# A layer norm, linear attention and gated MLP on one core: the first stage with column halves, another order of loads, and four h chunks begun on two token tiles

## The chip, the core and the metric

The kernel runs on one core of a Trainium2 chip. The metric is the device time of one execution in microseconds. Seven runs of the kernel before gave a median of 143.49 us, from 143.22 to 143.72.

## The reference

x has 2048 tokens of 448 features, all in bfloat16. The function normalises each token and sends the result through two branches. Branch A is linear attention with 16 heads of 28 features. Branch B is an MLP with 1792 hidden features and a squared ReLU. The output is x plus A times the SiLU of B.

```python
def _layernorm(x, axis=-1, eps=1e-5):
    m = jnp.mean(x, axis=axis, keepdims=True)
    v = jnp.var(x, axis=axis, keepdims=True)
    return (x - m) / jnp.sqrt(v + eps)
...
    qkv = (xn @ wqkv).reshape(B, S, 3, H, Dh)      # H = 16, Dh = 28
    phi = lambda t: jnp.where(t > 0, t + 1, jnp.exp(t)) + 1e-6
    pq, pk = phi(q), phi(k)
    kv = jnp.einsum("bhsd,bhse->bhde", pk, v)
    z = jnp.einsum("bhsd->bhd", pk)
    num = jnp.einsum("bhqd,bhde->bhqe", pq, kv)
    den = jnp.einsum("bhqd,bhd->bhq", pq, z)[..., None] + 1e-6
    s = (num / den).reshape(B, S, D) @ wo
...
    h = xn @ w1 + b1
    h = jnp.where(h > 0, h, 0) ** 2
    g = silu(h @ w2 + b2)
    return x + s * g
```

## The kernel before

**Tiles.** The 2048 tokens are 16 tiles of 128, in four groups of 512. The 448 features lie in four chunks of 128, 128, 128 and 64. Matmuls contract over features, so the normalised x (`xn`, tokens on partitions) is turned into `xT` (features on partitions). The last 64 features stand twice, on partitions 0 to 63 and 64 to 127, so that the half-height step of one product can run on either half of TensorE beside a step of another product. For this, `xn` has 512 columns: a copy, the twin (`ln_twin`, L477), puts columns 384 to 447 again into 448 to 511.

**Products of the first stage.** K is a product for one token tile (`kk`, matmuls at L597): 128 tokens by 512 of the columns of wqkv, from the k columns and the last of q. Q is one chunk of 128 q columns by a group of 512 tokens (`qq`, L628). H is one of 14 chunks of 128 hidden features by a group of 512 tokens (`hh`, L640). Each collects in one PSUM bank of 512 float32 columns, of which there are eight. K and Q go through phi: an Exp on ScalarE (L575) and two VectorE operations (L578, L585). H goes through ReLU with bias on ScalarE (L649) and a square on VectorE or ScalarE (L657, L658). `pe_four` runs four products in pairs of half-height matmuls, one of the pair on partitions 0 to 63 and the other on 64 to 127. Seven such half-height steps make one product, since the four chunks hold seven halves.

**Order of the work.** The program lists operations with what they read and write. `schedule` places them in planned time, and `emit` writes out one instruction stream for each engine, with semaphore waits for the true dependences and for reuse of PSUM banks. TensorE and SP keep the order of the program. ScalarE, VectorE and POOL take what can start soonest; among those near in start, the one with the smallest `late` goes first. `late` is the latest planned start, less `lead` for a DMA, or `prio` where it is set by hand. At run time each engine executes its stream strictly in order, so an instruction that waits holds all that stand behind it.

**The head.** Group 0 has its own code. `load_x(0, 1, "act")` issues the first x tile on ScalarE's queue, `load_x(1, 2)` the second on SP, and `load_x(2, 4, "act")` tiles 2 and 3 on ScalarE's queue. The weights for K (`load_k`: one main part for the first three chunks, two small rests for the fourth chunk and its copy) go on SP behind tile 1, then w1 columns 0 to 511 (`w1a`), x tiles 4 to 7, `w1b`, wq, `w1c`. The bias b1 is loaded as 14 rows of 128 on ScalarE's queue, and the activation table is loaded there after the DMA issues. Each tile then passes statistics (L444), aggregate (L447), Ln and Exp on ScalarE (L455, L459), which make the reciprocal deviation `rstd`, and the norm (L466). Priorities give VectorE the order in `order` (L996).

TensorE first runs ten matmuls of 512 columns on a zeroed tile `junk` (`warm`). `pe_transpose` turns a whole tile with five transposes and one copy out of PSUM, by ScalarE for tiles 0 and 2 and by VectorE for 1 and 3. `pe_two` gives the full-height steps of K0 and K1, then the transposes of tiles 2 and 3, then the two half-height rests of K0 and K1. b1 is turned after that, and `quads` starts with H0 H1 H2 H3:

```python
        streams = (
            ("H0 H1 H2 H3 K2 H4 K3 H6", "H5 Q0 Q1 H7 H8 H9 Q2 H11 H10 K0' H12 H13"),
```

K0' is the K product of tile 4, the first of the next group. Tiles 4 to 15 are turned by transposing DMAs on SP (`dma_transpose`, L505), and x of tiles 8 to 11 is loaded between those of tiles 5 and 6.

**Behind the first stage** come the last H products, the sums over tokens, the folds of the small matrices, and the second products with w2 and the attention output, group by group (L905, L971); the change edits none of it.

Of the kernel before, what the change touches and what calls it, by code (L numbers as in the profile page):

```python
# [9 lines left out]
P = 128  # L10
# [7 lines left out]
RATE = 262e3  # L18
LEAD = 8.0
# [13 lines left out]
class Op:  # L33
    def __init__(self, eng, emit, reads, writes, dur, alts, nbytes):
        self.eng, self.emit, self.dur, self.alts, self.nbytes = eng, emit, dur, alts, nbytes
        self.reads, self.writes = list(reads), list(writes)
        self.raw, self.deps, self.succ = set(), set(), []
        self.start = self.end = None
        self.seq = None
        self.late = 1e9  # L40
        self.lead = LEAD
        self.prio = None
        self.sync = set()
# [10 lines left out]
class Program:  # L54
# [3 lines left out]
    ENGINES = ("pe", "act", "dve", "pool", "sp")  # L58
# [27 lines left out]
    def schedule(self):  # L86
# [25 lines left out]
        free["pool"] = free["dve"] = 0.8  # L112
# [7 lines left out]
        def ready(op):  # L120
            r = 0.0
            for d in op.deps:
                if d.end is None:
                    return None
                r = max(r, d.end + (0.0 if d.eng == op.eng == "pe" and d not in op.sync else LAT))
            return r
# [14 lines left out]
        while n:  # L141
# [69 lines left out]
            if op.nbytes:  # L211
                free[e] = st + op.dur
                s2 = max(dma_free, st + 1.9)
                dma_free = s2 + op.nbytes / RATE
                op.end = dma_free + 0.7
            else:
                op.end = st + du
                free[e] = op.end
# [62 lines left out]
def bass_recurrent_scan__linear_attn_block__dense_activation_squared_relu__prompt_kernel(  # L281
    nc, A_x, A_wqkv, A_wo, B_x, B_w1, B_b1, B_w2, B_b2, out
):
    with ExitStack() as es:
# [5 lines left out]
        junk = sb("junk", [P, 512], bf)  # L290
# [14 lines left out]
        b1r = sb("b1r", [NF, P], bf)  # L305
# [33 lines left out]
        def pool(fn, writes, reads=(), dur=0.3):  # L339
            add("pool", fn, reads, writes, dur)  # L340
# [4 lines left out]
        add("dve", lambda e, _: e.memset(junk[:, :], 0.0), [], ["junk"], 0.2).prio = -1000  # L345
# [29 lines left out]
        pool(lambda e, _: e.memset(zmask[:, :, :], 1.0), ["zmask"])  # L375
# [22 lines left out]
        def load_k(eng, w, src, name, lo, hi, eng2=None):  # L398

            n = (hi - lo) * 2  # L400
            dma(
                eng, w[:, 0:3, lo:hi], src[0:384, lo:hi].rearrange("(c p) j -> p c j", p=P), [(name, 0)], 384 * n
            )
            for i in (0, 1):
                dma(eng2 or eng, w[64 * i : 64 * i + 64, 3, lo:hi], src[384:448, lo:hi], [(name, 1 + i)], 64 * n)

# [13 lines left out]
        load_x(0, 1, "act")  # L420
        load_x(1, 2)
        load_k("sp", w_qkv, A_wqkv, "wk", 384, 2 * D)
        load_x(2, 4, "act")
        dma("act", b1r[:, :], B_b1.rearrange("(f p) -> f p", p=P), ["b1r"], F * 2).prio = -103
# [5 lines left out]
        add("act", lambda e, _: e.preload_act_table_set("natural_log_exp_and_others"), [], ["actw"], 1.3).prio = -101  # L430

# [10 lines left out]
        def ln_stats(si, prio=(None, None)):  # L442
            add(
                "dve", lambda e, _: e.bn_stats(st6[:, si, :], x_tok[:, si, :]), [("x", si)], [("st", si)], 0.553  # L444
            ).prio = prio[0]
            add(
                "dve", lambda e, _: e.bn_aggr(mv[:, si, :], st6[:, si, :]), [("st", si)], [("mv", si)], 0.16  # L447
            ).prio = prio[1]

        def ln_rstd(lo, hi):  # L450
            c = slice(lo, hi)
            ts = range(lo, hi)
            add(
                "act",
                lambda e, _: e.activation(out=vep[:, c], in_=mv[:, c, 1], func=AF.Ln, bias=eps5[:, 0:1]),  # L455
                [("mv", i) for i in ts] + ["eps5", "actw"], [("vep", i) for i in ts], 0.2,
            )
            add(
                "act", lambda e, _: e.activation(out=rstd[:, c], in_=vep[:, c], func=AF.Exp, scale=-0.5),  # L459
                [("vep", i) for i in ts], [("rstd", i) for i in ts], 0.2,  # L460
            )

        def ln_norm(si, prio=None):
            add(
                "dve",
                lambda e, _: e.tensor_scalar(  # L466
                    out=xn[:, si, 0:D], in0=x_tok[:, si, :], scalar1=mv[:, si, 0:1],
                    scalar2=rstd[:, si : si + 1], op0=ALU.subtract, op1=ALU.mult,
                ),
                [("x", si), ("mv", si), ("rstd", si)], [("xn", si)], 0.43,  # L470
            ).prio = prio

        def ln_twin(lo, hi):

            ts = range(lo, hi)
            add(
                "dve", lambda e, _: e.tensor_copy(xn[:, lo:hi, 448:512], xn[:, lo:hi, 384:448]), [("xn", i) for i in ts],  # L477
                [("xd", i) for i in ts], 0.1 + 0.03 * (hi - lo),
            )

        def pe_transpose(si, eng, prio):
            b = Buf("T")

            def f(e, _):
                v = ps(b)[:, :].bitcast(bf)
                for c in range(3):
                    e.transpose(v[:, c * P : (c + 1) * P], xn[:, si, c * P : (c + 1) * P], ident[:, :])  # L487
                e.transpose(v[0:64, 3 * P : 4 * P], xn[:, si, 384:448], ident[:, :])  # L488
                return e.transpose(v[64:P, 3 * P : 4 * P], xn[:, si, 384:448], ident[:, :])

            add("pe", f, [("xn", si), "ident"], [b], 0.35)

            def ev(e, _):
                src = ps(b)[:, 0:256].bitcast(bf).rearrange("p (c k) -> p c k", c=4)
                dst = xT[:, :, si * P : (si + 1) * P]
# [4 lines left out]
            add(eng, ev, [b], [("xT", si)], 0.42 if eng == "dve" else 0.6).prio = prio  # L500

        def dma_transpose(si):
# [5 lines left out]
            op.lead = LEAD + STAGGER * (3 - si % 4)  # L508
# [43 lines left out]
        def pe_two(a, b, between):  # L552

            for u in (a, b):

                def f(e, _, u=u):
                    for k in range(3):
                        last = u.mm(e, 2, k, k == 0, False)
                    return last

                add("pe", f, u.reads, [u.bank], 3 * MM(u.n))
            between()

            def rest(e, _):
                a.mm(e, 0, 3, False, True)
                return b.mm(e, 1, 3, False, True)

            add("pe", rest, [r for u in (a, b) for r in [*u.reads, u.bank]], [a.bank, b.bank], MM(a.n) + 0.1)
            a.out()
            b.out()  # L570
# [20 lines left out]
        def kk(si):  # L591
# [10 lines left out]
            return Acc(b, [("xT", si)] + wnames("wk"), mm, lambda: phi(b, qk_of(si), ("pk", si), blocks), 512)  # L602
# [21 lines left out]
        def qq(g, m):  # L624
# [8 lines left out]
            reads = [("xT", 4 * g + i) for i in range(4)] + wnames("wq")  # L633
            return Acc(b, reads, mm, lambda: phi(b, pqT[:, m, g * 512 : (g + 1) * 512], ("pq", g, m), lambda a: a), 512)

        def hh(g, fi):
            b = Buf("H")

            def mm(e, h, c, start, stop):
                return e.matmul(  # L640
                    ps(b)[:, 0:512], w_1[half[h], c, fi * P : (fi + 1) * P], xT[half[h], c, g * 512 : (g + 1) * 512],
# [3 lines left out]
            def out():  # L645
# [9 lines left out]
                def sq(e, eng):  # L655
                    if eng == "dve":
# [5 lines left out]
            return Acc(b, [("xT", 4 * g + i) for i in range(4)] + wnames(w1_of(fi)), mm, out, 512)  # L662
# [333 lines left out]
        order = ["st0", "mv0", "st1", "mv1", "xn0", "st2", "xn1", "mv2", "st3", "mv3", "xT1", "xn2", "xn3", "xT2", "xT3"]  # L996
        at_head = {n: -100 + i for i, n in enumerate(order)}
        for si in range(4):
            ln_stats(si, (at_head[f"st{si}"], at_head[f"mv{si}"]))
            ln_rstd(si, si + 1)  # L1000
            ln_norm(si, at_head[f"xn{si}"])

        def warm(n, after=(), wide=False):
            b = Buf("W")

            def f(e, _):
                last = None
                for _i in range(n):
                    w = 512 if wide else P
# [3 lines left out]
            add("pe", f, ["junk", *after], [b], n * (0.426 if wide else 0.107))  # L1013
            return b

        warm(10, wide=True)
        pe_transpose(0, "act", -100)
        warm(2)
        pe_transpose(1, "dve", at_head["xT1"])

        def third_and_fourth():
            pe_transpose(2, "act", -100)
            pe_transpose(3, "dve", at_head["xT3"])

        pe_two(kk(0), kk(1), third_and_fourth)
        bb = Buf("B1")
        add(
            "pe", lambda e, _: e.transpose(ps(bb)[:, 0 : NF // 2].bitcast(bf), b1r[:, :], ident[0:NF, 0:NF]),
            ["b1r", "ident"], [bb], 0.1,
        )  # L1030
        add(
            "act", lambda e, _: e.activation(out=b1f[:, :], in_=ps(bb)[:, 0 : NF // 2].bitcast(bf), func=AF.Copy), [bb],
            ["b1f"], 0.25,
        )

        def quads(g, what):
# [11 lines left out]
            ("H0 H1 H2 H3 K2 H4 K3 H6", "H5 Q0 Q1 H7 H8 H9 Q2 H11 H10 K0' H12 H13"),  # L1048
# [4 lines left out]
        for g, (first, second) in enumerate(streams):  # L1053
            if g + 1 < NG:
                ln(4 * g + 4, 4 * g + 8)
            quads(g, first)
# [91 lines left out]
```

## Time and profile before

| | |
|---|---|
| median of seven runs | 143.49 us |
| the profiled execution, whole time | 143.22 us |
| the profiled execution, span | 142.0 us |
| TensorE busy | 137.8 us, 97% of the span |
| VectorE busy | 91.3 us, 64% |
| ScalarE busy | 78.7 us, 55% |
| x tile of 112 KB, ScalarE's queue and SP's, issue to landing | 2.7 and 2.6 us |
| x tiles 2 and 3, 224 KB, issue to landing | 3.8 us |
| K weights, main part of 384 KB; rests of 64 KB | 4.2 us; 4.1 us |
| w1a, main part of 384 KB | 4.1 us |
| first statistics start | 3.57 us |
| first transposes of tiles 0, 1, 2, 3 start | 5.49, 6.32, 8.10, 8.54 us |
| first matmul of K0 | 6.77 us |
| first matmul of H0 | 9.59 us |
| first matmul of K2 | 12.62 us |

Times inside the execution count from the start of the span. The whole time is longer than the span by what lies around the program's instructions. Busy time is the sum over an engine's instructions; a busy engine may still be off the path that sets the end. The granted clock of TensorE was full in all 40 slices of the span.

### The profile page before, as it was taken

To read this page: it belongs to the slowest core of one execution; us is meant where nothing else is said; L and a number is where in the kernel's file an instruction comes from. 1 tells how busy PE (TensorE), PEld (TensorE's weight loads), DVE (VectorE), ACT (ScalarE), POOL (GpSimd) and SP (SyncE) were. 2 spreads that over 40 slices of the span, in tenths; PEclk is the share of its full clock that TensorE was granted. 3 is DMA by queue.
4 is the path that set the end of the run, shared out by engine and by line. 5 is a ranking of instruction groups with operands and counts; after the bars stand their busy time and mean duration, and the time that the engine had idled before them with its cause. 6 is when DMAs were issued, how large, how long until landed. Compare 5 with 4: busy or idle time off the path is not lost.

```text
span 142.0 us, 3024 instructions
## 1 busy us (share of the span) xinstructions
PE 137.8 (97%) x1215; PEld 67.3 (47%) x1215; DVE 91.3 (64%) x218; ACT 78.7 (55%) x151; POOL 23.4 (17%) x37
## 2 busy tenths in 40 slices
PE   6999999999999999999999999999999999999992
PEld 2344444444444444444445455654555555555482
DVE  0979698698897999678959900149852436052743
ACT  3667979889878898879799572143030211030220
POOL 6000000000000000000790000000050507350670
PEclk9999999999999999999999999999999999999999
DMA  4998958999251300000000025990001110201022
GB/s 108 323 329 241 96 157 279 342 242 132 55 42 37 74 18 5 0 9 14 0 0 0 0 78 143 191 174 12 5 7 58 37 32 32 97 28 41 32 97 67
DMA packets 19809, 12.90 MB, mean 91 GB/s; under 512 B 9364, under 2 KB 19412, under 8 KB 19796
## 3 DMA queue, kind: packets, MB, share of 16 engines
q1 hardware_dynamic: 17644, 11.22, 33.2%
q10 hardware_dynamic: 2152, 1.50, 4.5%
q8 instruction: 9, 0.15, 0.4%
q14 instruction: 4, 0.03, 0.1%
HBM read 8.78 MB, written 2.10 MB: 77 GB/s over the span
## 4 chain that ended last, share of the span: by engine, by line
PE 93%; DVE 3%; DMA 2%; issue 0%; DVEq 0%
PE pb L905 30%; PE pb L640 30%; PE pb L597 8%; PE pb L971 8%; PE pb L672 6%; PE pb L628 6%; DMA x_tok<-in_A_x_dram 2%; DVE st L444 1%; PE pb L678 1%; PE pb L765 1%; PE pb L726 1%; PE pb L487 1%; PE pb L803 0%; DVE xn L466 0%; PE pb L488 0%; DVE xT L497 0%
## 5 line engine op out<-in xcount | busy, mean ns | idle before, releaser
L640 PE MATMUL pb<-xT,w 64*128 64x512 bf16 x392 | 50.8, 376 | 0.1
L905 PE MATMUL pb<-w,r 64*128 64x448 bf16 (+3 forms) x378 | 45.1, 343 | 0.0
L649 ACT ACTIVATE r<-pb,b1f 128x512 bf16<-128x512 f32 x56 | 34.9, 689 | 4.1 <-PE pb L640 4.1
L640 PEld LDWEIGHTS pb<-xT,w 64*128 64x128 bf16 x392 | 21.4, 94 | 23.3 <-ACT r L649 0.6
L905 PEld LDWEIGHTS pb<-w,r 64*128 64x128 bf16 (+1 forms) x378 | 22.7, 95 | 20.0 <-issue 1.2
L916 DVE TENSOR_TENSOR gbuf<-pb,b2b 128x448 bf16<-128x448 f32 (+1 forms) x16 | 9.3, 609 | 33.2 <-PE pb L905 33.2
L881 ACT ACTIVATE gbuf<-gbuf 128x448 bf16<-128x448 bf16 (+1 forms) x16 | 8.6, 564 | 37.1 <-DVE gbuf L916 34.4
L950 POOL TENSOR_TENSOR xn<-xn,x_tok 128x448 bf16<-128x448 bf16 x15 | 15.1, 1030 | 48.7 <-DVE xn L941 48.7
L597 PE MATMUL pb<-w_qkv,xT 64*128 64x512 bf16 (+1 forms) x106 | 17.6, 377 | 0.0
L628 PE MATMUL pb<-xT,w_qkv 64*128 64x512 bf16 x84 | 15.5, 376 | 0.0
L657 DVE TENSOR_TENSOR r<-r 128x512 bf16<-128x512 bf16 x38 | 13.2, 418 | 0.0
L382 POOL MEMSET kvm<- 128x2048 bf16 x1 | 1.8, 1804 | 64.9 <-DVE zb L622 64.9
L971 PE MATMUL pb<-msb,pqT 64*128 64x448 bf16 (+3 forms) x93 | 11.2, 343 | 0.0
L444 DVE BATCH_NORM_STATS2 st<-x_tok 128x6 f32<-128x448 bf16 x16 | 9.4, 612 | 2.4 <-DMA x_tok<-in_A_x_dram 2.4
L575 ACT ACTIVATE qk<-pb 128x512 bf16<-128x512 f32 x16 | 9.0, 594 | 3.3 <-PE pb L597 2.7
L585 DVE SCALAR_TENSOR_TENSOR qk<-pb,qk 128x512 bf16<-128x512 f32 x16 | 10.7, 687 | 0.2
L941 DVE TENSOR_TENSOR xn<-pb,gbuf 128x448 bf16<-128x448 f32 (+2 forms) x17 | 9.3, 590 | 1.9 <-ACT gbuf L881 1.5
L658 ACT ACTIVATE r<-r 128x512 bf16<-128x512 bf16 x18 | 10.4, 651 | 0.0
L597 PEld LDWEIGHTS pb<-w_qkv,xT 64*128 64x128 bf16 (+1 forms) x106 | 6.6, 94 | 6.5 <-DVE xT L497 0.3
L672 PE MATMUL pb<-qk,xn 128*128 128x448 bf16 x48 | 9.4, 352 | 0.0
L628 PEld LDWEIGHTS pb<-xT,w_qkv 64*128 64x128 bf16 x84 | 6.0, 94 | 5.0
L616 DVE TENSOR_TENSOR zacc<-zacc,qk 128x448 f32<-128x448 f32 x13 | 8.1, 622 | 0.3
(81 smaller groups left out, 98.6 us busy)
## 6 DMA issues: line engine op xcount, KB each, us to landing
out_dram<-xn SPq DMA_DIRECT2D x15, 112.0 KB, 1.7
w<-in_B_w_dram SPq DMA_DIRECT2D x1, 1568.0 KB, 9.6
x_tok<-in_A_x_dram SPq DMA_DIRECT2D x3, 448.0 KB, 4.2
w<-in_B_w_dram SPq DMA_DIRECT2D x2, 384.0 KB, 4.6
xT<-rows ACTq DMA_DIRECT2D x6, 112.0 KB
w<-in_B_w_dram SPq DMA_DIRECT2D x1, 576.0 KB, 5.5
xT<-rows SPq DMA_DIRECT2D x5, 112.0 KB
w_o<-in_A_wo_dram SPq DMA_DIRECT2D x1, 392.0 KB, 10.7
```

What stands on the lines that cost most here:

```text
L444: "dve", lambda e, _: e.bn_stats(st6[:, si, :], x_tok[:, si, :]), [("x", si)], [("st", si)], 0.553
L585: lambda e, _: e.scalar_tensor_tensor(out=slot, in0=src(), scalar=1.0 + 1e-6, in1=slot, op0=ALU.add, op1=ALU.max),
L597: return e.matmul(ps(b)[:, 0:512], xT[half[h], c, si * P : (si + 1) * P], w_qkv[half[h], c, 384 : 2 * D], start=start, stop=stop,)
L628: return e.matmul(ps(b)[:, 0:512], w_qkv[half[h], c, m * P : (m + 1) * P], xT[half[h], c, g * 512 : (g + 1) * 512], start=start, stop=stop,)
L640: return e.matmul(ps(b)[:, 0:512], w_1[half[h], c, fi * P : (fi + 1) * P], xT[half[h], c, g * 512 : (g + 1) * 512], start=start, stop=stop,)
L649: lambda e, _: e.activation(out=slot, in_=ps(b)[:, 0:512], func=AF.Relu, bias=b1f[:, fi : fi + 1]),
L657: return e.tensor_tensor(out=slot, in0=slot, in1=slot, op=ALU.mult)
L658: return e.activation(out=slot, in_=slot, func=AF.Square)
L672: last = e.matmul(ps(b)[:, 0:D], xn[:, si, c * P : (c + 1) * P], pk_of(si), start=(si == 0), stop=(si == NT - 1),)
L905: return e.matmul(ps(b)[:, 0:n], r2[half[h], fi, si * P : (si + 1) * P], w_2[half[h], fi, c], start=start, stop=stop)
L950: eng, lambda e, _: e.tensor_tensor(out=ob, in0=ob, in1=x_tok[:, si, c], op=ALU.add),
L971: return e.matmul(ps(b)[:, 0:n], q, m, start=start, stop=stop)
```

## The change

It edits the head, the planner's constants, and the planned place of some operations.

- **Loads.** x tiles 0, 1 and 2-3 are all issued on SP, in this order. On ScalarE's queue come the activation table, then b1, then the main part of the K weights, which waits for `ident`; the two rests of the K weights are issued on SP. All else on SP follows as before.
- **Halves.** The norm of tiles 0 to 3 is done in two parts, of columns 0 to 255 and 256 to 447, each tile followed by its own twin. Transposes take chunks of 128 columns, the fourth with its twin, so a tile has four in place of five. For tiles 0, 1 and 3 two chunks each are copied out of PSUM in one operation; tile 2 is copied whole.
- **TensorE's order.** b1 is turned first after the warm-up, as a full 128 by 128 square, for which POOL zeroes `b1r`. The full-height steps of K0 and K1 stand between the transposes of tiles 0 and 1. H0 to H3 each run on tokens 0 to 255 first (`first`), with full-height steps for three chunks (`mains`) and paired half-height steps for the fourth (`rests`), around the transposes of tiles 2 and 3. Their other 256 tokens (`second`) go into the same banks with `pe_four`.
- **The warm-up** reads a constant of ones made at the start of the program in place of `junk`.
- **Planning.** The head's VectorE and ScalarE operations get a fixed order through `after`. `after` delays an operation in the plan alone; it adds no wait. phi of K0 and K1 is planned behind the head, as are the mask operations of POOL and the statistics of tiles 4 to 7. `lead` of the transposing DMAs of tiles 4 to 7 goes from 17, 14, 11 and 8 to 8.2, 6.8, 5.4 and 4. The assumed DMA rate and latencies change.

```diff
-RATE = 262e3
+RATE = 300e3
...
+            if any(d.end is None for d in op.after):
+                return None
...
-                s2 = max(dma_free, st + 1.9)
+                s2 = max(dma_free, st + 1.75)
                 dma_free = s2 + op.nbytes / RATE
-                op.end = dma_free + 0.7
+                op.end = dma_free + 0.3
...
-        load_x(0, 1, "act")
+        table = add("act", lambda e, _: e.preload_act_table_set("natural_log_exp_and_others"), [], ["actw"], 1.3)
+        table.prio = -120
+        load_x(0, 1)
         load_x(1, 2)
-        load_k("sp", w_qkv, A_wqkv, "wk", 384, 2 * D)
-        load_x(2, 4, "act")
-        dma("act", b1r[:, :], B_b1.rearrange("(f p) -> f p", p=P), ["b1r"], F * 2).prio = -103
+        load_x(2, 4)
+        dma("act", b1r[0:NF, :], B_b1.rearrange("(f p) -> f p", p=P), ["b1r"], F * 2, ["b1r"]).prio = -115
+        load_k("act", w_qkv, A_wqkv, "wk", 384, 2 * D, "sp", ["ident"]).prio = -110
...
+            c = slice(0, D) if part is None else (slice(0, 256), slice(256, D))[part]
...
+            chunks = range(4) if part is None else (2 * part, 2 * part + 1)
+            for i, c in enumerate(chunks):
+                reads = [("xn", si, c // 2)] if c < 3 else [("xd", si)]
+                add(
+                    "pe",
+                    lambda e, _, i=i, c=c: e.transpose(
+                        ps(b)[:, i * 64 : (i + 1) * 64].bitcast(bf), xn[:, si, c * P : (c + 1) * P], ident[:, :]
+                    ),
+                    reads + ["ident"] + ([b] if i else []), [b], 0.1,
+                )
...
+            op.lead = LEAD + STAGGER * (3 - si % 4) if si > 7 else 4.0 + 1.4 * (7 - si)
...
+        def mains(u, ks=K3, reads=None):
+            def f(e, _):
+                for k in ks:
+                    last = u.mm(e, 2, k, k == 0, False)
+                return last
...
+        def rests(lo, hi):
+            def f(e, _):
+                lo.mm(e, 0, 3, False, True)
+                return hi.mm(e, 1, 3, False, True)
...
         warm(10, wide=True)
...
+        add("pe", lambda e, _: e.transpose(b1v(), b1r[:, :], ident[:, :]), ["b1r", "ident"], [bb], 0.1)
...
+        k0, k1 = kk(0), kk(1)
+        first = [hh(0, fi, 0) for fi in range(4)]
+        second = [hh(0, fi, 1, first[fi].bank) for fi in range(4)]
...
+        turn(0, 0, "act")
+        turn(0, 1, "act")
+        turn(1, 0, "act")
+        mains(k0, (0, 1), [("xT", 0, 0)] + wnames("wk")[:1])
+        turn(1, 1, "dve")
+        mains(k0, (2,), [("xT", 0, 1)])
+        k_mains(k1, 1)
+        mains(first[0])
+        rests(k0, k1)
...
+        mains(first[1])
+        head["xT2"] = pe_transpose(2, None, "act")
+        mains(first[2])
+        turn(3, 0, "act")
+        turn(3, 1, "dve")
+        mains(first[3])
+        rests(first[0], first[2])
+        rests(first[1], first[3])
+        for eng, names in (
+            ("dve", "st0 mv0 st1 mv1 xn00 xn01 xd0 xn10 xn11 xd1 st2 mv2 xT11 st3 mv3 xn20 xn21 xd2 xn30 xn31 xd3 xT31"),
+            ("act", "ln0 ex0 ln1 ex1 b1 xT00 xT01 xT10 ln2 ex2 ln3 ex3 xT2 xT30"),
+        ):
...
+        pe_four(*second)
...
-            ("H0 H1 H2 H3 K2 H4 K3 H6", "H5 Q0 Q1 H7 H8 H9 Q2 H11 H10 K0' H12 H13"),
+            ("K2 H4 K3 H6", "H5 Q0 Q1 H7 H8 H9 Q2 H11 H10 K0' H12 H13"),
```

In the names, `xn01` is tile 0, second half; `xd` is the twin; `xT11` is the copy out of PSUM of tile 1, second half; `st`, `mv`, `ln` and `ex` are the statistics, the aggregate, Ln and Exp.

## The prediction

> **What bounds the kernel.** I read the shares of the span first, then the chain of waits.
>
> ```profile
> PE 137.8 (97%) x1215; PEld 67.3 (47%) x1215; DVE 91.3 (64%) x218; ACT 78.7 (55%) x151; POOL 23.4 (17%) x37
> ...
> PE 93%; DVE 3%; DMA 2%; issue 0%; DVEq 0%
> ```
>
> The second line is the chain that ends last: TensorE has 93% of it, and the rest is mostly its first stretch. The same chain in order of time (start, length, what) shows it:
>
> ```profile
> 0.80 2.75 DMA x_tok<-in_A_x_dram
> ...
> 3.57 0.64 DVE st L444
> ...
> 5.15 0.28 DVE xn L466
> 5.43 0.54 DVE st L444
> 5.96 0.31 DVE xn L466
> ...
> 6.83 1.43 PE pb L597 x6
> ...
> 9.10 0.44 DVE xT L497
> ...
> 9.59 3.20 PE pb L640 x28
> ```
>
> Up to 9.59 us the chain goes through the x load and VectorE; from there no two TensorE matmuls start more than 0.23 us apart until 71.4. So the change is worth what it moves one mark: the start of K2, the first work that is the same in both kernels. Here K2 starts at 12.62 in the timeline, after 28 matmuls of H0 to H3 from 9.59, so these take 3.04. The stretch behind it leaves the helpers this room (TensorE, weight loads, VectorE, ScalarE, POOL busy):
>
> ```profile
> 9.60:71.40 61.80, 61.80 (x574) 27.74 (x574) 53.28 (x134) 51.65 (x100) 3.06 (x3) 1.00 0.50 105
> ```
>
> VectorE is 86% busy and ScalarE 84%: TensorE is the limit, with 8.5 us to spare on VectorE.
>
> **The loads.** All of x 0-3 now goes on SP, in order; the main part of wk goes on ScalarE's queue behind the table load and b1, and waits for `ident`.
>
> ```profile
> 2.48 1.28 ACT L430 ACT_TABLE_LOAD   x1 [2.48 <-issue]
> ...
> 82.92 0.54 ACT L690 ACTIVATE at<-pb 128x448 bf16<-128x448 f32 x1 [0.28 <-PE pb L678]
> 82.92 1.24 ACTq L393 DMA_DIRECT2D tiles<-rden  x2
> ```
>
> SP's issues take 0.39 to 0.6 each, 0.04 apart: x0 0.81, x1 1.25, x2-3 1.67, two wk rests, w1a main 3.35 (2.95 now). Every later SP issue slips the same 0.40. The first two x tiles now land together, 2.7 and 2.6 after issue on two queues; x0 first on its queue shares less. Bounds: 3.57 for the first statistics (no gain), and 3.10 (112 KB at the 375 GB/s moved from 4.5 to 5.0 take 0.3, so 0.3 off the 2.6, with rounding). I take s = 3.25. x1 is in by 1.25+2.6 = 3.85, needed at s+0.76; x2-3 by 1.67+3.8 = 5.5, needed at s+2.76.
>
> wk main: a DMA issue started in the same instant as an ACTIVATE in the last two lines above, so issue need not wait for the engine. No row shows it beside a table load. If it passes: b1 at 1.0 to 1.7 (its 0.70), wk at 1.8 (`ident` ends at 1.56 now, about 0.2 later with the b1 memset ahead on POOL), landing 1.8 + 4.2 = 6.0 at most. If it is held for the 1.28: table 0.8 to 2.08, b1 to 2.8, wk at 2.85. I take the first, by the only row with both. The Trainium skill speaks against this order: its page "ScalarE: Activation LUTs", section "What ACT_TABLE_LOAD costs", has a drain of 1380 ns beside a 1283 ns load; the trace agrees on the load (1.28) and shows no drain, the ACTIVATE after it starting at 4.45 when VectorE's aggregate ended. Were an issue held for both, wk would be issued near 4.2 and land near 8.4, an estimate that would make the time some 144.9.
>
> **VectorE's order**, from starts in the timeline: statistics to aggregate 0.63 to 0.67, 0.09 more to the next; a whole norm (448 columns) holds the engine 0.29; norm of tile 0 starts 1.49 after its statistics, through Ln and Exp. A half norm: adds of 256 and 192 columns (L950) take 0.29 and 0.26, 0.47 ns a column, so halves hold it 0.19 and 0.16: +0.06 a tile (bounds 0 and +0.29, two whole ones). The one-tile twin waits for its norm half to be written (0.28) and takes 0.13, from 0.195 for two tiles (bounds 0.1 to 0.2). From s this gives: norms of tile 0 at 1.49 and 1.68, twin 1.96; tile 1 at 2.21 (its rstd: aggregate done 1.57, Ln 0.29, Exp 0.20), 2.40, twin 2.68; statistics 2 at 2.76, aggregate 3.39; copy xT11 3.48; statistics 3 at 3.67, aggregate 4.30; tile 2 at 4.39, 4.58, twin 4.86; tile 3 waits for rstd to 5.13, 5.32, twin 5.60; copy xT31 6.03 to 6.28. Four twins and halves cost more than half copies save: VectorE ends its head at 9.53, where it ends at 9.52 now.
>
> **TensorE's order.** Transposes start 0.06 apart and take 0.22; a 256-column full-array matmul costs 0.109 (1.53 for 14 at the end, L905). Half copies on ScalarE: 0.19 for 14 columns and 0.60 for 512 give 0.40 for 256. Transposes of tile 0 begin at s+1.80; b1 copied at 2.17; xT00 ends 2.70, xT01 2.97, xT10 3.24. k0 starts at 2.74, if wk main is in (s+2.74 = 5.99, so 6.0 just fits); T11 behind it ends at 3.45; k1 to 4.15; then H0's first half, the k rests, H1's first half to 5.01. Tile 2 waits for its twin (5.0), ends 5.4; the copy xT2 runs 5.43 to 6.03 and xT30 to 6.37. H3's first half needs a PSUM bank: K0, K1, H0, H1, H2 and three transposes hold all eight, so it waits for xT2, 6.07 to 6.39; rests to 6.60. The second halves take 3.04/2 = 1.52: K2 at s + 8.12 = 11.37, 1.25 before 12.62. What makes the gain is not an earlier last tile but 1.5 us of H work done while waiting for it.
>
> **Loss terms.** w1a main, issued 3.35, by its own 4.1 lands at 7.45, and H0 wants it at s+4.15 = 7.40; before, its use was at 9.59 and hid this. Everything in TensorE's order behind H0 waits with it: 0.10 (0 to 0.4). w1b (0.4 later, issue 5.79 + 5.2 = 11.0) is wanted by H4 at 12.2: nothing; w1's last part and wq have over 1 us too. VectorE reaches K2 with 1.84 us of time after its head in place of 3.1 (12.62 - 9.52), so 1.3 us more backlog (phi of K0 and K1, tiles 4 to 7), against 8.5 spare: 0.10 (0 to 0.5). The lower lead of the first transposed loads only makes tiles 4 to 7 less urgent; tile 7's lands at 18.99 + 2.5 = 21.5, and H0 of the next group starts near 25.8: some 3 us of cover even when the mark moves 1.2. Earlier warm-up matmuls (no wait for `junk`, 0.45) and POOL's memset lie in time in which TensorE waits for x anyway; the mask operations get only a planned place, no wait. Ten warm matmuls start 0.43 apart until 4.6, later ones of that size 0.216: should the slow rate return in the thin stretch behind them, k0 and k1 would cost up to 1.3 more; the equally thin stretch of now (5.4 to 6.8) shows no such return.
>
> Sum: 1.25 - 0.10 - 0.10 = 1.05. The profiled execution took 143.22 (span 142.0 and 1.2 around it), so 142.17; the median of the runs is 0.27 above it: **142.4** (142.0 to 143.0 with the bounds: s, the halves, both loss terms).
>
> **Rivals.**
> *The table load holds the queue, mildly (0.14).* wk issued at 2.85; by bytes it lands near 6.3, by its own 4.2 at 7.05: 0.3 to 1.06 past 5.99, one for one, since T11 stands behind k0 and VectorE's statistics of tile 3 behind xT11: 142.7 to 143.5, taken 143.0. For: no row of an issue beside a table load. Against: the ACTIVATE row.
> *The k weights come last of all (slower, 0.14).* Same place, but wk main shares the 16 engines with w1a main, issued 0.5 later, and takes the 5.2 that w1b's equal 384 KB took beside x: 2.85 + 5.2 = 8.05, 2.06 late: 144.5; half as late 143.5; taken 144.0. It decides from a landing at 7.04 (5.99 + 1.05). For: now wk is issued at 1.25 and has 0.5 us in hand. Against: bytes moved at 320 to 390 GB/s would have x and wk (0.98 MB) across by 5.2.
> *The gain goes back on TensorE (0.12).* Either banks run out behind the backlog, or the second halves go at the pace of weight loads: 28 by 94 ns is 2.63, +1.1: 143.5 (143.0 to 143.7). For: 94 ns a load, two in each 0.107 pair. Against: 16 loads and matmuls of L726 in 0.82, so loads overlap at 0.05.
>
> **Numbers.** Forecast 0.60, rivals 0.14, 0.14, 0.12. A measurement of this kernel tells about 0.2% (0.29 us) from no change. Faster: 0.60 + 0.10 + 0.03 = 0.73; same: 0.03 + 0.07 = 0.10; slower: 0.14 + 0.02 and 0.01 = 0.17. The range reaches from 141.9 (s = 3.1, no loss, and a little) to 143.7, leaving out most of the slower case.
>
> **What would show it.** First statistics at 3.1 to 3.4; an ACTq issue of wk at 1.8, beside the table load; k0 at about 6.0; xT31 near 9.5; the second H halves from 9.9 and 1.5 long; K2 near 11.4; no gap above 0.23 us after it. k0 past 7.0, or statistics of tile 3 past 7.9, would prove me wrong; so would matmul gaps between 11 and 20.

## The result and the profile after

The changed kernel took 144.30 us (median of 13 runs, 143.67 to 145.49), the kernel before 143.41 us (33 runs, 143.18 to 144.17). The ratio is 1.0073 (95% interval 1.0055 to 1.0091): slower by 0.7%, where the prediction had 142.4, faster. The spread tells as much: 1.8 us from the lowest run to the highest, where the kernel before has 1.0. Medians and ranges here are over all runs; ratios leave out single runs that lie over 1.5% above their kernel's fastest (one in e2, two in e3, one in e4, three in e10 below), and are not simply the ratios of the medians.

The profiled execution of the changed kernel took 143.73 us, with a span of 142.5. Its page, engines and the chain by engine:

```profile
PE 137.6 (97%) x1225; PEld 69.8 (49%) x1225; DVE 92.5 (65%) x227; ACT 78.1 (55%) x152; POOL 22.6 (16%) x38
...
PE 92%; DMA 3%; SPq 2%; DVE 0%; ACT 0%; issue 0%; DVEq 0%
```

VectorE has left the chain; DMA and SP's issues have taken its place. The chain in order of time (start, length, what):

```profile
3.42 0.59 SPq L396
...
4.60 3.97 DMA w<-in_B_w_dram
8.57 0.05 issue
8.62 0.50 PE pb L659 x3
9.12 0.32 PE pb L612 x2
...
10.14 0.61 ACT xT L512
10.74 0.05 issue
10.79 2.35 PE pb L659 x35
```

The head now waits for a weight: the last small part of w1a, issued at 4.60, lands at 8.57, and H0 starts at 8.62. The first matmul of K2 comes at 12.98, 0.36 later than before (12.62), where 11.37 was predicted. The two rows of K2 in the timelines, before and after:

```profile
12.62 1.03 PE L597 MATMUL pb<-w_qkv,xT 64*128 64x512 bf16 x8
...
12.98 1.03 PE L612 MATMUL pb<-w_qkv,xT 64*128 64x512 bf16 x8
```

The timeline of the head (start, length, engine, line, operation; in brackets the engine's idle time before it and what ended that):

```profile
0.80 1.28 ACT L425 ACT_TABLE_LOAD   x1 [0.80 <-PEq L1191]
...
1.03 0.64 ACTq L396 DMA_DIRECT2D b1r<-in_B_b_dram  x1
...
1.72 0.45 ACTq L396 DMA_DIRECT2D w_qkv<-in_A_wqkv_dram  x1
...
2.95 0.63 DVE L449 BATCH_NORM_STATS2 st<-x_tok 128x6 f32<-128x448 bf16 x1 [2.95 <-DMA x_tok<-in_A_x_dram]
...
6.79 0.59 PE L612 MATMUL pb<-w_qkv,xT 128*128 128x512 bf16 x2 [0.99 <-DMA w_qkv<-in_A_wqkv_dram]
```

Two DMA issues start inside the table load (0.80 to 2.08), so the queue is not held by it. The first statistics start at 2.95, as x0 lands, 0.6 earlier than before. K0 waits 0.99 for the main part of wk, issued at 1.72 and 4.9 in landing. What the DMA engines moved meanwhile, the windows show (stretch, length, busy times of the engines, granted clock, DMA share, GB/s). Before:

```profile
3.00:3.50 0.50, 0.50 (x3) 0.22 (x2) 0.00 (x0) 0.50 (x1) 0.26 (x2) 1.00 0.85 239
3.50:4.00 0.50, 0.50 (x3) 0.17 (x2) 0.43 (x1) 0.26 (x1) 0.00 (x0) 1.00 1.05 390
```

After:

```profile
3.00:3.50 0.50, 0.50 (x3) 0.23 (x2) 0.50 (x1) 0.00 (x0) 0.41 (x2) 1.00 0.47 32
3.50:4.00 0.50, 0.50 (x3) 0.16 (x2) 0.47 (x3) 0.17 (x1) 0.22 (x2) 1.00 0.77 205
```

There is a hole in the traffic: two x tiles of 112 KB and the small b1 were all that was issued by 1.7, where the kernel before had 832 KB issued by then (112 + 112 + 384 + 224). Half a microsecond at 32 in place of 239 GB/s, and another at 205 in place of 390, are some 200 KB that every later load is behind. Whether this hole is what delays wk is another question: the experiments below do not bear it out.

The head is not all of it. From the first product with w2 to the first attention output, both on TensorE, the kernel before has 27.41 us (the two rows below), and the changed kernel 27.54:

```profile
71.66 0.93 PE L905 MATMUL pb<-w,r 128*128 128x448 bf16 x4
...
99.07 0.35 PE L971 MATMUL pb<-msb,pqR 64*128 64x448 bf16 x2
```

VectorE before that output in the kernel before:

```profile
95.19 0.62 DVE L916 TENSOR_TENSOR gbuf<-pb,b2b 128x448 bf16<-128x448 f32 x1 [1.76 <-PE pb L905]
95.95 1.19 DVE L776 CAST msb<-pb 128x448 bf16<-128x448 f32 x2
97.28 0.96 DVE L866 TENSOR_TENSOR pqT<-pqT,xT 128x1536 bf16<-128x1536 bf16 x1
```

VectorE and TensorE in the changed kernel:

```profile
72.02 0.55 PE L926 MATMUL pb<-w,r 128*128 128x448 bf16 x2
...
96.75 0.96 DVE L887 TENSOR_TENSOR pqT<-pqT,xT 128x1536 bf16<-128x1536 bf16 x1 [2.96 <-DMA xT<-rows]
97.62 0.28 DVE L893 TENSOR_TENSOR pqR<-pqR,xT 128x256 bf16<-128x256 bf16 x1
97.83 0.62 DVE L937 TENSOR_TENSOR gbuf<-pb,b2b 128x448 bf16<-128x448 f32 x1
98.36 1.15 DVE L797 CAST msb<-pb 128x448 bf16<-128x448 f32 x2
...
99.56 0.36 PE L992 MATMUL pb<-msb,pqR 64*128 64x448 bf16 x2
```

The order on VectorE has turned round, in code that the change does not edit. The product of pqT with the reciprocal denominators waits for the DMAs that replicate these; it now stands ahead of the bias add and the two msb copies, which wait for no DMA. VectorE idles 2.96 us at it, the copies end at 99.51, and TensorE's first attention output, which reads msb, comes 27.54 after the first w2 product. In this execution that costs 0.13; with 0.36 in the head it makes the 0.5 that this profile is slower (143.73 against 143.22). The median is another 0.57 above this profile, so other executions are slower still. Six of the profiles below (e1, e3, e4, e7, e8, e11) have the turned order too. In these seven the product starts 24.39 to 25.79 us after the first w2 product, as the DMAs land, and the attention output comes 27.41 to 28.60 after it, the later the later. So the order costs between nothing and 1.2 us from profile to profile, by how late those DMAs land.

### The profile page after: what moved, and what is told of

Its sections match the earlier page's. It is cut to its first block, busy times and chain, and to the rows that moved or that the text cites. A ratio compares the mean times of both kernels' runs of the same rounds, so it can differ in the third digit from the quotient of the medians.

```text
span 142.5 us, 3056 instructions
## 1 busy us (share of the span) xinstructions
PE 137.6 (97%) x1225; PEld 69.8 (49%) x1225; DVE 92.5 (65%) x227; ACT 78.1 (55%) x152; POOL 22.6 (16%) x38
## 4 chain that ended last, share of the span: by engine, by line
PE 92%; DMA 3%; SPq 2%; DVE 0%; ACT 0%; issue 0%; DVEq 0%
PE pb L926 30%; PE pb L659 30%; PE pb L992 8%; PE pb L612 8%; PE pb L693 6%; PE pb L643 6%; DMA w<-in_B_w_dram 3%; SPq L396 2%; PE pb L699 1%; PE pb L786 1%; PE pb L747 1%; PE pb L824 0%; ACT xT L512 0%; DVE xn L962 0%; PE pb L817 0%
## 5 line engine op out<-in xcount | busy, mean ns | idle before, releaser
L659 PE MATMUL pb<-xT,w 64*128 64x512 bf16 (+2 forms) x408 | 51.5, 365 | 0.4 <-DMA w<-in_B_w_dram 0.3
L659 PEld LDWEIGHTS pb<-xT,w 64*128 64x128 bf16 (+1 forms) x408 | 23.7, 94 | 22.1 <-DMA w<-in_B_w_dram 0.6
L676 DVE TENSOR_TENSOR r<-r 128x512 bf16<-128x512 bf16 x40 | 13.8, 418 | 0.0
L677 ACT ACTIVATE r<-r 128x512 bf16<-128x512 bf16 x16 | 9.1, 652 | 0.0
L590 ACT ACTIVATE pqT<-pb 128x512 bf16<-128x512 f32 x12 | 6.8, 597 | 3.7 <-PE pb L659 2.1
```

The lines of the kernel that those rows point to most:

```text
L590: add("act", lambda e, _: e.activation(out=slot, in_=src(), func=AF.Exp), [buf, "actw"], [tile], 0.6)
L659: return e.matmul(ps(b)[:, c0 : c0 + n], w_1[half[h], c, fi * P : (fi + 1) * P], xT[half[h], c, t : t + n], start=start, stop=stop,)
L676: return e.tensor_tensor(out=slot, in0=slot, in1=slot, op=ALU.mult)
```

## The experiments

Theory W was that the weights' landings bind a head that is good in itself; theory C that the halves, twins and their order cost more than they bring. After the first four, theory P came in: the planner's new constants turn VectorE's order round. The table reads each profile by the same marks: start of the first statistics, of K0, H0 and K2, and the time from the first w2 product to the first attention output (stage two). Times are medians over all runs (6 to 13 of each kernel, 29 to 35 of the one before); ratios are to the kernel before, run beside it. e1 to e8 ran on one chip and e9 to e12 on another; the medians of the kernel before lie between 143.41 and 143.47 throughout.

| kernel | stats | K0 | H0 | K2 | stage two | median | range | ratio, interval |
|---|---|---|---|---|---|---|---|---|
| before | 3.57 | 6.77 | 9.59 | 12.62 | 27.41 | 143.41 | 143.18-144.17 | |
| after | 2.95 | 6.79 | 8.62 | 12.98 | 27.54 | 144.30 | 143.67-145.49 | 1.0073 (1.0055-1.0091) |
| e1 | 3.74 | 6.44 | 8.02 | 12.44 | 28.11 | 143.85 | 142.96-144.94 | 1.0026 (0.9999-1.0053) |
| e2 | 2.99 | 7.61 | 10.43 | 13.46 | 27.41 | 144.01 | 143.67-146.30 | 1.0050 (1.0026-1.0074) |
| e3 | 3.48 | 6.92 | 8.43 | 12.79 | 27.41 | 143.65 | 143.31-145.92 | 1.0017 (0.9993-1.0041) |
| e4 | 2.93 | 6.46 | 8.18 | 12.54 | 27.59 | 143.87 | 143.21-145.72 | 1.0039 (1.0012-1.0066) |
| e5 | 2.96 | 6.88 | 8.97 | 13.33 | 27.41 | 143.74 | 143.24-143.94 | 1.0014 (0.9999-1.0028) |
| e6 | 3.60 | 6.31 | 7.88 | 12.24 | 27.41 | 142.95 | 142.81-143.66 | 0.9971 (0.9959-0.9984) |
| e7 | 3.70 | 6.96 | 9.78 | 12.81 | 28.42 | 144.59 | 143.95-145.32 | 1.0081 (1.0054-1.0107) |
| e8 | 2.98 | 6.24 | 7.66 | 12.01 | 28.60 | 143.59 | 142.93-144.72 | 1.0015 (0.9991-1.0039) |
| e9 | 3.71 | 6.54 | 8.45 | 12.81 | 27.41 | 143.39 | 143.01-143.90 | 0.9992 (0.9980-1.0005) |
| e10 | 3.14 | 7.61 | 10.36 | 14.83 | 27.41 | 145.70 | 143.65-147.08 | 1.0121 (1.0091-1.0151) |
| e11 | 3.84 | 6.54 | 8.02 | 12.37 | 28.20 | 143.74 | 143.28-145.05 | 1.0027 (1.0004-1.0051) |
| e12 | 2.92 | 6.33 | 8.44 | 12.80 | 27.41 | 143.41 | 143.12-143.83 | 0.9996 (0.9984-1.0007) |

From K2 to the first w2 product all profiles have 59.02 to 59.05, but for e4 with 59.23; from the first attention output to the end of the span they have 42.87 to 42.92, but for e4 with 43.74. So the first stage passes on the start that it gets, and profiles differ by their K2 and their stage two alone.

### The loads apart from the rearranged work

**e1_old_loads.**

```diff
-        load_x(0, 1)
+        load_x(0, 1, "act").prio = -130
         load_x(1, 2)
-        load_x(2, 4)
-        load_k("act", w_qkv, A_wqkv, "wk", 384, 2 * D, "sp", ["ident"]).prio = -110
+        load_k("sp", w_qkv, A_wqkv, "wk", 384, 2 * D)
+        load_x(2, 4, "act").prio = -125
...
         rests(k0, k1)
+        bb = Buf("B1")
...
+        add("pe", lambda e, _: e.transpose(b1v(), b1r[:, :], ident[:, :]), ["b1r", "ident"], [bb], 0.1)
```

(the table load behind the two x issues, b1's transpose and copy behind the K rests, as in the kernel before)

> The changed kernel with the loads as before: x0 and x2-3 on ScalarE's queue, x1 and all of wk on SP, and b1 (which then lands late) turned behind the K rests. Theory W (the weights' landings bind the new head, the rearranged work itself is good): x0 lands 3.5, wk main about 5.5, w1a complete about 7.7; K0 starts near 6.3 and waits for no load, H0 near 7.8, K2 between 11.6 and 12.1, time 142.4 to 143.0. Theory C (the halves, twins and their order cost more than they bring): K2 at 12.6 or later, time 143.4 or more.

K0 and H0 start 0.1 and 0.2 later than expected, and K2 at 12.44 lies between the two bounds: the old loads bring 0.54 back, but not all that was hoped. And the time is 143.85 with 2 us of spread; in the profile stage two takes 28.11, so 0.7 is lost there, by the same turned order. This profile made theory P.

**e2_new_loads.** The kernel before with the loads of the changed one (the same lines as in the change).

> The kernel before with the loads of the changed one alone: x all on SP, table load, b1 and the main part of wk on ScalarE's queue. Theory W: the wk parts land at 6.6 to 7.1, K0 starts at 7.1 in place of 6.77 and all behind it shifts; w1a at 8.6 is still in time for H0; K2 at 12.8 to 13.2, time 143.6 to 144.2. Theory C: x lands 0.6 earlier and the loads are good: K2 at 12.6 or earlier, time 143.4 or less.

Slower by 0.5%, as theory W has it, but by a wait that it did not name. The page's timeline has K0 late because of VectorE, not of wk:

```profile
6.17 0.63 DVE L445 BATCH_NORM_STATS2 st<-x_tok 128x6 f32<-128x448 bf16 x1 [1.34 <-DMA x_tok<-in_A_x_dram]
```

x2-3, third on SP, lands 4.43 after its issue at 1.72, and the old order on VectorE has the statistics of tile 2 ahead of the norm of tile 1. The wait of theory W is close behind: K0 needs all of wk here, the last part landed at 7.44, and K0 started at 7.61.

**e3_wk_first.**

```diff
-        load_k("act", w_qkv, A_wqkv, "wk", 384, 2 * D, "sp", ["ident"]).prio = -110
+        load_k("act", w_qkv, A_wqkv, "wk", 384, 2 * D, "sp").prio = -118
```

> The changed kernel with wk main issued ahead of b1 on ScalarE's queue and without the wait for ident: issue near 0.9 in place of 1.72. Theory W1 (late because of late issue, with the DMA engines idle from 3.0 to 3.6): the hole is filled, wk main lands at 5.2 to 5.9, w1a complete by 8.2, x0 some 0.2 later; K2 12.2 to 12.6, time 143.3 to 143.8. Theory W2 (late because two queues share the engines turn by turn): wk main lands after 6.4 again, K2 near 13.0, time 144.1 to 144.4.

Issued at 0.83, 0.9 earlier, wk main lands at 4.62, 2.0 earlier, so it was late by late issue (W1) and not by turn-sharing alone (W2). But now x pays: x0 lands at 3.46 and x1 at 4.93, and VectorE's second statistics start when x1 lands. K2 comes at 12.79, later than W1 had it (12.2 to 12.6). Stage two is 27.41 here although the order is the turned one: the product came early enough.

**e4_w1a_main.**

```diff
-        mains(first[0])
+        def h_mains(u):
+            mains(u, K3, [n for n in u.reads if n[0] == "xT"] + [("w1a", 0)])
+
+        h_mains(first[0])
```

(the other three call it too)

> The changed kernel with the first H steps waiting for the main part of w1a alone, not for its two rests. Theory W: H0 starts at the landing of the main part, some 0.35 earlier (8.25 in place of 8.6), K2 0.2 to 0.35 earlier, time 143.9 to 144.1. Theory C: no change, 144.3.

H0 starts 0.44 earlier and K2 too (12.54), more than expected, 0.09 of it because w1a's main part landed at 8.14 here and at 8.23 in the changed kernel; the median, 143.87, lies just below the 143.9 to 144.1 expected. Stage one lost 0.18 of it at one TensorE wait for VectorE, from 13.40 to 13.58. This execution's span ends 0.8 later than its last matmul would have it, in the last store, which none of the marks takes in.

### The planner's constants

**e5_old_constants.**

```diff
-RATE = 300e3
+RATE = 262e3
...
-                s2 = max(dma_free, st + 1.75)
+                s2 = max(dma_free, st + 1.9)
...
-                op.end = dma_free + 0.3
+                op.end = dma_free + 0.7
```

> The changed kernel with the planner's constants as before (rate 262e3, 1.9, 0.7). Before the chip runs it, its VectorE order has the second bias add and the two msb copies ahead of the first pqT product again, as the kernel before has. Theory P (the new constants put a product that waits for a DMA ahead of work that TensorE needs at its first attention output): the head stays as in the changed kernel (K2 12.7 to 13.2), the time from the first w2 product to the first attention output returns to 27.4 in every profile, median 143.8 to 144.1, and the spread of the runs shrinks. Rival H (all the loss is the head's): no change, 144.3.

143.74, just below what was expected, stage two at 27.41, and a range of 0.7 in place of 1.8. K2 was late in this profile (13.33), and the profiled run was one of the slowest of its twelve (143.89).

**e7_before_new_constants.** The reverse edit, in the kernel before.

> The kernel before with the three planner constants of the change (rate 300e3, 1.75, 0.3) and nothing else. Theory P: K2 stays at 12.6; VectorE's first pqT product stands ahead of the bias add and the msb copies, and the first attention output waits for them in runs where the replicating DMAs land late: 27.4 to 28.1 from the first w2 product, median 143.5 to 143.9, more spread. Rival H: as before, 143.4 to 143.5.

The three numbers alone make the kernel before 0.8% slower, as much as the whole change does within the intervals, and more than expected. Its timeline:

```profile
97.46 0.96 DVE L866 TENSOR_TENSOR pqT<-pqT,xT 128x1536 bf16<-128x1536 bf16 x1 [3.84 <-DMA xT<-rows]
98.33 0.29 DVE L872 TENSOR_TENSOR pqR<-pqR,xT 128x256 bf16<-128x256 bf16 x1
98.53 0.62 DVE L916 TENSOR_TENSOR gbuf<-pb,b2b 128x448 bf16<-128x448 f32 x1
99.07 1.15 DVE L776 CAST msb<-pb 128x448 bf16<-128x448 f32 x2
...
100.27 0.36 PE L971 MATMUL pb<-msb,pqR 64*128 64x448 bf16 x2 [0.84 <-DVE msb L776]
```

VectorE stands 3.84 us at the product; TensorE waits for the copies and starts 1.0 later than its 27.41. The plan with the new constants puts the product where the replicating DMAs have not yet landed, and VectorE, which keeps its order, pays for that.

**e12_order_pinned.** The changed kernel with its new constants; only the plan holds the products back.

```diff
         store(15, [ca, cb], "act")
+        for op in scaled:
+            op.after = copies
         pr.schedule()
```

(`scaled` holds the pqT and pqR products, `copies` the msb copies)

> The changed kernel with its new constants and its loads; in the plan alone, the products of pqT and pqR come after the msb copies. If the constants cost time only by this order on VectorE: first attention output 27.4 after the first w2 product in every profile, time 143.6 to 143.9 as e5_old_constants, spread under 1 us. If they cost it elsewhere: 144.1 to 144.4.

143.41: less than expected, and equal to the kernel before (ratio 0.9996, 0.9984 to 1.0007). In the traces of this kernel and the changed one, VectorE's bias add and two msb copies stand elsewhere; all five engines otherwise have the same instructions in the same order. So the constants cost time by this order alone. The timeline has the old picture, with TensorE at 27.41:

```profile
95.38 0.62 DVE L938 TENSOR_TENSOR gbuf<-pb,b2b 128x448 bf16<-128x448 f32 x1 [1.76 <-PE pb L927]
96.14 1.19 DVE L797 CAST msb<-pb 128x448 bf16<-128x448 f32 x2
97.48 0.96 DVE L887 TENSOR_TENSOR pqT<-pqT,xT 128x1536 bf16<-128x1536 bf16 x1
```

So 0.89 of the median of the changed kernel (144.30 less 143.41) is this order; by e5, which turns it back in another way, 0.56. What is left, the head as it stands, is worth nothing by e12 and costs 0.33 by e5. The two have the same loads and the same head, but in their profiles wk main landed at 6.20 and 6.83 and K2 came at 12.80 and 13.33.

### What the head can bring

**e6_x23_act.** Old constants, the shorter wait of e4, and other loads:

```diff
         load_x(0, 1)
         load_x(1, 2)
-        load_x(2, 4)
+        load_x(2, 4, "act").prio = -118
...
-        load_k("act", w_qkv, A_wqkv, "wk", 384, 2 * D, "sp", ["ident"]).prio = -110
+        load_k("sp", w_qkv, A_wqkv, "wk", 384, 2 * D)
```

> The changed kernel with three edits: x2-3 alone on ScalarE's queue behind the table load, all of wk on SP behind x0 and x1; the first H steps wait for the main part of w1a alone; the planner's constants as before. Theory W plus P: four transfers are issued by 1.75, the hole in the DMA traffic is gone; x0 lands near 3.2, wk main 5.2 to 5.5, w1a main 7.0 to 7.3; K0 near 6.0, K2 at 11.6 to 12.0, second stage 27.4; time 142.5 to 142.9. Theory C: K2 12.4 or later, 143.3 or more.

142.95 and a ratio of 0.9971 (0.9959 to 0.9984): faster than both kernels, by 0.3% than the one before. Its chain waits for x and then for work; the one weight close to it is w1a's main part, which lands at 7.83 and holds H0 for some 0.1:

```profile
0.80 2.77 DMA x_tok<-in_A_x_dram
...
3.60 0.64 DVE st L449
...
9.39 0.61 ACT xT L512
10.00 0.05 issue
10.05 2.35 PE pb L659 x35
```

K2 at 12.24 is later than expected, by x0 (3.60, not 3.2) and by work: from the first statistics to K2 it takes 8.64, where the prediction's sum has 8.12; e1 has 8.70. From H0 to K2 alone it is 4.36 where the sum has 3.97, as in the changed kernel (8.62 to 12.98).

**e9_x23_act_alone.** e6 without the shorter wait.

> As e6_x23_act, but the first H steps wait for all of w1a again: the loads alone, with the planner's constants as before. Set beside e5_old_constants (143.74) it gives the price of the load order; beside e6_x23_act (142.95) that of the wait for the two w1a rests. Load theory: K0 6.0 to 6.4, H0 at the landing of the last w1a rest, 8.1 to 8.5, K2 12.4 to 12.8, time 143.1 to 143.4. If the wait for the rests were all of the gain of e6_x23_act: 143.6 or more.

143.39, and H0 starts as the last w1a rest lands (8.40). Set between e5 and e6 it would give the loads 0.35 of their 0.79 and the shorter wait 0.44. The first is not shown: e12, run beside e9, has the loads of e5, waits for all of w1a too, and has 143.41 with K2 at 12.80 (12.81 in e9). The shorter wait moves H0 from 8.45 to 7.88 and K2 by 0.57 between the profiles of e9 and e6.

**e11_x23_new_constants.** e6 with the new constants.

> As e6_x23_act, but with the planner's new constants (rate 300e3, 1.75, 0.3). Theory P: K2 near 12.2 as there, the first attention output again behind the product that waits for a DMA, 27.9 to 28.6 after the first w2 product in place of 27.4; time 143.5 to 144.1 and a spread of over 1 us. Rival: the constants cost only beside late heads, time 142.9 to 143.2.

143.74, stage two 28.20, range 1.8: as theory P has it. On the better head the constants take 0.79 (e6 ran on the other chip), all that it brings and more.

**e10_small_first.** e6 with one 64 KB wk rest first on ScalarE's queue, then x2-3, then b1.

```diff
-        load_x(2, 4)
+        k_rest("act", 0).prio = -119
+        load_x(2, 4, "act").prio = -118
```

> As e6_x23_act, with one 64 KB wk rest ahead of x2-3 on ScalarE's queue, so that x0 shares the DMA engines with less. If x0's landing still sets the head: x0 lands 3.1 to 3.3 in place of 3.57, K2 11.8 to 12.1, time 142.6 to 142.9. If w1a's landing (7.8) sets it: K2 near 12.2, time as e6_x23_act, 142.9 to 143.0.

Neither: 145.70. x0 did land at 3.12, but b1, third on its queue, landed 4.65 after its issue at 2.09, and TensorE's order has b1 first:

```profile
PEclk9959999999999999999999999999999999999999
...
6.79 0.23 PE L1049 MATMUL pb<-ident,b1r 128*128 128x128 bf16 x1 [2.20 <-DMA b1r<-in_B_b_dram]
...
8.65 1.49 PE L620 MATMUL pb<-w_qkv,xT 128*128 128x512 bf16 x3
```

The first line is the granted clock of the page in 40 slices: behind the idle stretch it falls to 5 tenths in the third slice, and K0 and K1 start a matmul every 0.427 in place of 0.216. K0 comes 1.30 later than in e6, and K2 2.59. Eight of the twelve runs have a granted clock of 0.987 or 0.988 over their span, the other four 0.999 or 1.000.

**e8_weights_not_loaded.** The changed kernel; wk and w1a are left out and filled with a constant by POOL.

```diff
-        load_w1("w1a", 0, 512)
+        pool(lambda e, _: e.memset(w_qkv[:, :, 384 : 2 * D], 0.01), [("wk", i) for i in range(3)], dur=1.8).prio = 50
+        pool(lambda e, _: e.memset(w_1[:, :, 0:512], 0.01), [("w1a", i) for i in range(3)], dur=1.8).prio = 51
```

> The changed kernel without the loads of wk and w1a; POOL fills both with a constant in their place, so K and H0 to H3 are computed from that constant. It shows the rearranged head with no weight to wait for. Theory W: first statistics 2.9 to 3.1, K0 near 5.8, H0 near 7.1, K2 at 11.2 to 11.7, time 142.1 to 142.9 (the second stage may take back up to 0.7). Theory C: K2 at 12.4 or later.

K2 at 12.01, between the theories, and muddied by its own fill: two half norms take 0.89 in this timeline beside POOL's 1.8 us memset, and 0.56 in the changed kernel. With stage two at 28.60 its time (143.59) says nothing of the head. What is left for theory C is the work between H0 and K2 that the sum lacks: 0.39 in the changed kernel and in e6.

## Why the prediction was wrong

The sum had 142.17 for a profile, and the changed kernel's profile has 143.73. Of the 1.56 between them, 1.41 is K2 (12.98, where the sum with its two loss terms comes to 11.57) and 0.13 is stage two. Over the runs the order of stage two costs more: without it the kernel has 143.41 (e12), which leaves 1.0 of the miss to the head and puts 0.89 on the order.

**A step that it does not have: the planner's constants.** The prediction prices the lower `lead` and passes over the assumed DMA rate and latencies, though the change lists them and the kernel's text says that VectorE takes what the plan lets start soonest. They were costed at nothing without a word. They are the 0.89 of e12 (0.56 by e5), and 1.18 in the kernel before (144.59 less 143.41, e7).

**The landing of wk** was put at "6.0 at most", by 1.8 + 4.2. The issue came at 1.72, beside the table load, as predicted. It took 4.9, landed near 6.7 and made K0 1.1 late (6.79 against 2.95 + 2.74 = 5.69). The 4.2 of the row was measured with the issue at 1.25, beside three x loads from two queues; with the changed loads it was not reached once: wk main took 4.5 (e12) to 5.4 us (e2). Late issue is shown to matter (e3: 0.9 earlier, landed 2.0 earlier). That the hole in the traffic is what makes it long is not shown, and the traces speak against it: from 3.0 to 3.5 e12 moves 34 GB/s and e6, without the hole, 372, and wk main takes 4.5 in both. The cause of the longer landing stays open. The rival with the late k weights had the right place, but blamed the table load.

**The landing of w1a** was weighed by its main part, 7.45, and priced at 0.10. The main part landed at 8.23, and H0 waits for all three parts, as the text of `mains` has it where no reads are given: 8.57. That is 0.42 of K2 on top of wk (H0 at 8.62 less 2.95 + 4.15 = 7.10, less the 1.10).

**The work of the head** was summed 0.4 too short. In the changed kernel H0, the K rests and H1 start at 8.62, 9.05 and 9.38: 0.43 and 0.33, where 0.33 and 0.215 were counted. Each turn between full-height and half-height matmuls goes with about 0.1 more, and the sum has three such turns without a price; the third, behind H3's first half, makes 0.43 of 0.33 again. That the turn itself is the reason is read from these gaps and not tested by a run. The Trainium skill's page "TensorEngine Tiling (Array Packing)", "Key Properties", says that a change of tiling mode drains TensorE. It gives no price; these gaps agree with it.

**Right** were the issue beside the table load, the half norms nearly (0.56 a pair; tile 0's first half starts 1.48 after its statistics, its twin 2.08, where 1.96 was summed), the bank wait in front of H3, the second halves at matmul pace rather than at 94 ns a load, and the first stage that passes its start on whole (59.04). x0 alone on its queue came at 2.95, better than the bound of 3.10, which was luck for the sum. The section "What ACT_TABLE_LOAD costs" of the Trainium skill's page "ScalarE: Activation LUTs" has a drain beside the load. That drain held no DMA back here: b1 was issued at 1.03 and wk at 1.72, both inside the load. Whether it runs before the next ACTIVATE, no run here shows, since that one starts 1.75 after the load. The cold clock, priced at up to 1.3, came up in the profile of e10 alone; one of the changed kernel's runs without a profile (145.43 us) also has a granted clock of 0.988, where the others have 0.999 or 1.000.

So K2 was forecast 1.25 earlier and came 0.36 later: 1.52 by weights that land late (0.10 of it priced), 0.39 by work that was not counted, less 0.30 for the earlier x0; and what stage two takes lies on top. None of the signs that were to prove the prediction wrong came up: K0 stayed under 7.0, the statistics of tile 3 (7.74) under 7.9, and no gap over 0.23 us lies between matmuls from 11 to 20. They watched the landing of wk and the backlog; none watched w1a's rests, the turns or stage two. The range was also narrow by its own terms: with s at 3.57 and both losses at their upper ends the sum comes to 143.5, not 143.0.

## What to carry to other kernels

Where a planner orders in-order engines, a constant of its model is an edit of every engine's order: compare the whole order before and after, and look for instructions that wait for a DMA and have moved ahead of ones that do not. A load's time holds for the traffic that it was measured in; when issues move, add up what has been issued by when on all queues, and take for each wait the last part that it names. Where an instruction on the path waits for a DMA, the runs spread as its landings do: 1.8 us in the changed kernel, 0.7 with the order pinned (e12).

## What was not expected of the hardware

- One queue issuing DMAs 0.45 us apart does not keep the DMA engines busy at first: 250 GB/s from 2.5 to 3.0, then 32 to 3.5, with the next two issued at 1.72. (e12 has 234 and 34.) It need not cost time: e12 is as fast as e9, which loads from two queues.
- b1 of 3.5 KB landed in 2.06 when issued first on its queue (1.03 to 3.09), and in 4.65 when issued third there.
- A turn from half-height to full-height matmuls or back goes with a gap of about 0.1 us on TensorE (0.43 and 0.33 for 0.33 and 0.215 of matmuls).
- The same loads in the same order land differently from execution to execution: wk main at 6.20, 6.33, 6.66 and 6.83 in e12, e4, the changed kernel and e5, all issued at 1.71 or 1.72.
- VectorE's half norms beside a POOL memset took 0.89 a pair in place of 0.56 (e8).
